# Second recurrence of a recurrent-memory attention and MLP gradient: rows loaded for two row groups at a time, one store of a block's gradient rows, and a new table of order

## The chip, the core and the metric

The kernel runs on one core of a Trainium2 chip. The metric is the time of one execution on the device in microseconds (us); the time before is 2793.9 us, the median of three runs (2793.06 to 2796.42). Below, PE is TensorE, ACT is ScalarE, DVE is VectorE, POOL is GpSimd, and SP is SyncE, whose queue issues nearly all of the transfers here. A trailing q (SPq) means the queue of that engine.

## The reference

The forward pass is a sum of a recurrent-memory attention and an MLP, both fed by the layer-normed input; the kernel returns the output and the gradients of ten inputs.

```
def _A_ref(x, mem0, Wq, Wk, Wv, Wo, seg_len):      # S 2048, Dm 512, H 32, Dh 128, M 8, seg 32
    mem = mem0
    for s in range(n_seg):                          # 64 segments, one after another
        h = jnp.concatenate([mem, x[:, s * seg_len:(s + 1) * seg_len, :]], axis=1)
        q, k, v = (jnp.einsum('btd,dhe->bhte', h, W) for W in (Wq, Wk, Wv))
        scores = jnp.where(mask, jnp.einsum('bhqe,bhke->bhqk', q, k) * scale, -1e9)
        o = jnp.einsum('bhqk,bhke->bhqe', _softmax(scores), v)
        o = jnp.einsum('bhte,hed->btd', o, Wo)
        mem = o[:, :M, :]
        outs.append(o[:, M:, :])
def _B_ref(x, w1, b1, w2, b2):                      # F 1792
    h = jnp.einsum('bsd,df->bsf', x, w1) + b1
    return jnp.einsum('bsf,fd->bsd', jnp.where(h > 0, h, 0) ** 2, w2) + b2
xn = _layernorm(x)
out = x + _A_ref(xn, ...) + _B_ref(xn, ...)
# returned: out and the vector-Jacobian product of out with grad_out, for all ten float inputs
```

The gradient runs through the 64 segments backwards, since the gradient of a segment's memory rows is a part of the gradient of the segment before.

## The kernel before

The program has four stages. The MLP with its gradients comes first; then the first recurrence (64 segments forwards); then the **second recurrence**, which walks the segments backwards and is the stage that the change touches; then the gradients of the attention weights (line 2159), a long run of matmuls over activations that the recurrences stored to DRAM.

In the second recurrence four segments make a block, and there are 16 blocks. For each segment there is a *step* (`chain`, called once for each segment) and `load`, which fetches the next segment's stored probabilities and activations. A step projects the incoming gradient rows (`proj`, line 864, weights `WB`, rows `PA`), forms three block-diagonal products (`bd_half`, line 974) whose results go through `XK`, multiplies them by the weights (`dh_part`, line 1774, weights `WA`) into the bank `R_A` (a slice of `XN`), and hands the memory rows to the next step by a small matmul, `gm` (line 1989), and a copy into `PA` (line 1992). So a step's last operations are: the last matmul of line 1774, the copy of the bank into `XN` on ACT (line 756), `gm`, the copy on DVE into `PA`, and the first `proj` of the next step. That loop through all 64 steps is the chain; all else in the stage is off it.

Each product of line 974 is evicted into `XK` by ACT or DVE (lines 756, 754), stored by SP as `S_GN<-XK`, turned on DVE (line 847) and read by line 1774. There are two buffers for three such products a step, so the third eviction of a step waits until the first one's store has landed.

Off the chain, once in a block, stand `l_pre` (lines 1809 and 930 are its matmuls, and line 864 with `PB`) and `l_post`. `l_post` goes over four row groups r, twice: it loads rows of `S_Q` (then of `S_GON`) and a padded table `S_DSL` (then `S_PL`) for each r (`load_x`), and multiplies two groups at a time (`mm`, line 1874). `blk_out` turns the block's gradient rows and stores them from `gNat` (a view of the tile `maskL`) to `S_GOA`.

Nothing is scheduled while the program runs. Every operation of the stage has a number in a table (`_BWD`, three tuples: the middle blocks, the first, the last), its due time in a block in nanoseconds times four, plus the engine that does it where there is a choice. `_Beat.run` sorts by these numbers, and each engine takes its instructions strictly in that order. SP too: a transfer that waits holds up every transfer behind it. A transfer takes one of eight semaphores in turn, so at most eight of SP's are under way.

Of the kernel before, what the change touches and what calls it, by code (L numbers as in the profile page):

```python
# [17 lines left out]
P = 128  # L18
# [179 lines left out]
        -546000, -2857200, -480000, -481200, 8879250, 1958400, 3563600, 3428400, 3358800, 10119849, 10143660,  # L198
        10143673, 10758308, 10758321, 6099600, 4994800, 2060400, 541200, 4580802, 7385202, 7385602, 8326802, 8824402,
        9103200, 9060400, 12611600, 12610400, 13626861, 13626873, -4334000, -3086798, -8438400, -12837600, -319597,  # L200
        -13471197, -16186000, 938000, 14389648, 14697884, 15015510, 15015520, 15015546, 15015568, 14915540, 14915552,
        14915565, 15155304, 15155317, 16495172, 12582691, 12582703, 14416771, 12582715, 12178775, 12178787, 12178799,
        13008887, 15015532, 15015557, 15015580, 15015593, 15246942, 16495186, 15246952, 15246964, 17158024, 17158036,
        15015664, 15015606, 16401514, 16401526, 16401538, 16401550, 16401562, 16401622, 16495198, 16495210, 17240374,
        17240386, 18255066, 17240398, 18255078, 15015619, 15015631, 15015643, 15015655, 16401575, 16401585, 16401597,
        16401611, 16944336, 16944349, 17240410, 17240423, 17240433, 17240446, 17240456, 17240517, 18235906, 18286922,
        18235916, 18235928, 18286932, 18286944, 23428480, 16401635, 16401645, 16401657, 16401671, 16401681, 16401693,
        16401707, 16401717, 17232288, 17783157, 17240469, 17240481, 17240493, 17240507, 18255090, 18255102, 18255114,
        18255127, 18255136, 18977533, 18569534, 18977546, 18569544, 18569556, 18977568, 18977580, 18977556, 19690537,
        19782597, 19690548, 19690562, 19782608, 19782622, 24547084, 17535616, 28380764, 13327536, 14420532, 24402643,  # L210
        24402655, 22194524, 19977928, -2821228, 7899676, 7373828, 3613352, -4696608, 8571312, 11740568, -69781,
        1558124, 4805860, 6352296, 7315404, 7733381, 10119800, 10119812, 10119824, 10119836, 2902029, 11447020,
        11447032, 11447044, 11447056, 11447070, 11447082, 12669054, 12669066, 13626802, 13626812, 13626824, 13626836,
        13626848, 13626884, 20930640, 20930652, 20930665, 23601096, 23601110, 24402664, 21843516, 21843528, 21843541,
        25147548, 25147561, 26802176, 18255151, 18255163, 23864939, 18255175, 20385003, 19204219, 17240531, 19148035,
        23864948, 23864961, 24748972, 24748985, 24715950, 26802190, 26947188, 27003728, 27104816, 27104828, 24749044,
        24402678, 25646686, 25646698, 25646710, 25646722, 25646734, 25646794, 26802202, 26802214, 26802226, 26802238,
        26802250, 26985338, 26802310, 24748999, 24749011, 24749023, 24749035, 25646747, 25646757, 25646769, 25646783,
        28361976, 28361989, 26802263, 26802275, 26802285, 26802297, 28614648, 28614661, 28362002, 28614710, 29609052,
        29609064, 29609076, 29609088, 30713416, 25646807, 25646817, 25646829, 25646843, 25646853, 25646865, 25646877,  # L220
        25646889, 27878264, 28843061, 27878278, 27878291, 27878301, 27878314, 26802321, 27541630, 26802335, 27083430,
        29000060, 29000073, 28843074, 29000146, 29609100, 29609112, 29609124, 29609136, 29000156, 29609149, 29609161,
        29609172, 29609210, 29609184, 29609222, 29609196, 25929872, 28805088, 21959012, 27793388, 30828719, 30828731,
        28733856, 29000084, 29609232, 29609244, 29609257, 31001308, 32005190, 32005200, 30458968, 31138912, 31138925,
        32272300, 32272313, 33163544, 29000099, 29000111, 29000123, 29000135, 28614675, 28614687, 28614699, 32237603,
        32237612, 32237637, 32237624, 32237649, 33139906, 33315202, 33982864, 33982876, 34779744, 34779756, 32237708,
        32281674, 32281686, 32281698, 32281710, 32281722, 32281734, 32281794, 33163558, 33163570, 33163582, 33163594,
        33810362, 33757294, 33810374, 32237663, 32237675, 32237687, 32237699, 32281747, 32281757, 32281769, 32281783,
        34296780, 34296793, 33163607, 33163619, 33163631, 33163641, 34923492, 34923505, 34296806, 34923566, 35592576,
        35621428, 35621440, 35621452, 35407824, 32281805, 32281817, 32281831, 32281843, 32359965, 32281853, 32281865,  # L230
        32281879, 34313164, 34989221, 34313177, 34313191, 34313201, 34313215, 33810386, 33810398, 33810410, 33810422,
# [1990 lines left out]
```

## Time and profile before

| What | Value |
|---|---|
| Median of three runs | 2793.9 us (2793.06 to 2796.42) |
| The profiled execution, its own time | 2801.72 us |
| Its span, first to last instruction | 2799.9 us |
| ACT busy in the whole span | 1288.3 us (46%) |
| DVE busy in the whole span | 1501.0 us (54%) |
| POOL busy in the whole span | 937.8 us (33%) |
| Bytes moved by transfers | 607.92 MB |
| Mean granted TensorE clock | 0.995 |

The times of the profile are from one execution, which took 7.8 us more than the median of the others. A busy share says how long an engine worked, not whether its waits matter: an idle engine costs something only where the engine that sets the end waits for it. In a row of waits the columns are the sum in us, how often, and the longest. In a row of a chain of waits they are the start in us, the length in us, and what held the chain there. In a row that groups instructions the columns behind the bar are busy us, mean ns of one, and the idle time before them with what ended it.

### The profile page before, as it was taken

How to read it: one execution, taken by the hardware profiler on the slowest of the kernel's cores; microseconds unless marked ns; L12 is line 12 of the kernel's file. 1: busy time of each engine (PE TensorE's matmuls, PEld its weight loads, DVE VectorE, ACT ScalarE, POOL GpSimd, SP SyncE). 2: the span in 40 equal slices, each digit the busy share in tenths (PEclk: the TensorE clock that was granted, in tenths of full speed). 3: DMA queues.
4: the chain of work that ended last, by engine and by line, in shares of the span. 5: the costliest groups of instructions: out<-in, count | busy, mean ns of one | idle time of the engine just before them, and what ended most of it. 6: DMA issues, size and time to landing. Idle time of an engine off the chain costs nothing.

```text
span 2799.9 us, 113515 instructions
## 1 busy us (share of the span) xinstructions
PE 2676.2 (96%) x47433; PEld 1560.2 (56%) x47617; DVE 1501.0 (54%) x4483; ACT 1288.3 (46%) x3070; POOL 937.8 (33%) x2624
## 2 busy tenths in 40 slices
PE   9999999999999998899999999999999899999999
PEld 7664566666666665655555555555555444444444
DVE  6555666666666666765555555555655402232322
ACT  4333555555555555556666666666666400000000
POOL 1103333233332333345444444454544301112211
PEclk9999999999999999999999999999999999999999
DMA  8748788788887764567989999989989898788861
GB/s 234 235 145 225 195 209 212 204 202 214 211 210 204 203 200 154 154 166 219 236 227 237 224 234 241 230 227 237 231 239 220 250 348 270 231 256 270 257 184 40
DMA packets 560278, 607.92 MB, mean 217 GB/s; under 512 B 231940, under 2 KB 361364, under 8 KB 557716
## 3 DMA queue, kind: packets, MB, share of 16 engines
q1 hardware_dynamic: 544580, 546.57, 73.0%
q0 software_dynamic: 15184, 54.08, 6.3%
q8 instruction: 373, 6.11, 1.0%
q14 instruction: 141, 1.16, 0.2%
HBM read 290.27 MB, written 272.12 MB: 201 GB/s over the span
## 4 chain that ended last, share of the span: by engine, by line
PE 43%; issue 7%; DMA 5%; DVE 2%; ACT 2%; POOL 1%; SPq 0%; POOLq 0%; ACTq 0%; DVEq 0%
PE ps L1774 13%; PE ps L2159 12%; PE ps L974 6%; PE ps L864 6%; PE ps L750 2%; DMA S_GN<-XK 2%; PE ps L1989 1%; DMA WA<-S_GN 1%; PE ps L1874 1%; PE ps L1934 1%; ACT XN L756 1%; PE ps L930 1%; DMA S_GNL<-dLN 0%; PE ps L1861 0%; POOL out_dram L2172 0%
## 5 line engine op out<-in xcount | busy, mean ns | idle before, releaser
L864 PE MATMUL ps<-WA,PA 128*32 128x512 bf16 x6144 | 367.9, 379 | 6.2 <-issue 2.9
L2159 PE MATMUL ps<-WA,WB 128*128 128x512 bf16 x1505 | 330.7, 379 | 2.2 <-DVE gwo L754 0.6
L1774 PE MATMUL ps<-WA,XK 128*32 128x512 bf16 x5120 | 307.1, 382 | 10.2 <-DVE XK L847 9.5
L864 PEld LDWEIGHTS <-PA 128*32 128x32 bf16 x8192 | 202.8, 96 | 196.1 <-DVE PA L1992 12.4
L2159 PEld LDWEIGHTS <-WB 128*128 128x128 bf16 x1896 | 185.5, 98 | 224.7 <-issue 0.9
L756 ACT CAST gwo<-ps 128x512 bf16<-128x512 f32 x64 | 33.2, 598 | 518.0 <-PE ps L2159 357.8
L990 POOL COPY BDA<-PB 32x128 bf16<-32x128 bf16 x538 | 155.9, 290 | 306.6 <-DVE PB L1563 253.1
L754 DVE CAST gwo<-ps 128x512 bf16<-128x512 f32 x64 | 40.0, 685 | 402.4 <-PE ps L2159 267.9
L756 ACT CAST XK<-ps 128x512 bf16<-128x512 f32 x379 | 211.0, 589 | 88.1 <-PE ps L974 65.8
L1774 PEld LDWEIGHTS <-XK 128*32 128x32 bf16 x5120 | 122.5, 97 | 146.2 <-DVE XK L847 31.1
L1774 PE MATMUL ps<-WA,XN 128*32 128x512 bf16 x2560 | 174.1, 381 | 2.4 <-DVE XN L847 2.1
L2170 POOL DMA_DIRECT2D out_dram<-gwo x96 | 71.4, 751 | 296.1 <-ACT gwo L756 264.3
L756 ACT CAST XA<-ps 128x512 bf16<-128x512 f32 x143 | 83.7, 590 | 151.3 <-PE ps L864 142.3
L756 ACT COPY XN<-ps 128x256 f32<-128x256 f32 (+2 forms) x215 | 93.6, 465 | 125.4 <-PE ps L1774 122.5
L864 PE MATMUL ps<-WB,PA 128*32 128x512 bf16 x2048 | 134.4, 385 | 10.0 <-issue 4.7
L847 DVE STREAM_TRANSPOSE XK<-XK 128x256 f32<-128x256 f32 x256 | 112.2, 442 | 44.6 <-ACT XK L756 38.6
L1432 PE MATMUL ps<-WB,OT 128*32 128x256 bf16 x4096 | 132.9, 275 | 3.2 <-DVE OT L847 1.6
L990 POOL COPY BDB<-PB 32x128 bf16<-32x128 bf16 x279 | 80.0, 287 | 163.5 <-DVE PB L1564 142.7
L990 ACT COPY BDA<-PB 32x128 bf16<-32x128 bf16 x430 | 127.1, 295 | 16.6 <-DVE PB L1563 7.6
L756 ACT CAST kN<-ps 128x512 bf16<-128x512 f32 x124 | 72.8, 587 | 128.5 <-PE ps L864 104.0
L996 POOL COPY BDA<-XA 32x256 bf16<-32x256 bf16 x256 | 104.5, 408 | 54.1 <-ACT BDA L990 17.1
L974 PEld LDWEIGHTS <-XK 128*128 128x128 bf16 x1536 | 94.5, 98 | 46.3 <-issue 15.9
(308 smaller groups left out, 5493.7 us busy)
## 6 DMA issues: line engine op xcount, KB each, us to landing
S_GN<-XK SPq DMA_DIRECT2D x192, 256.0 KB
WA<-S_GN SPq DMA_DIRECT2D x160, 256.0 KB
S_Q<-qN SPq DMA_DIRECT2D x64, 256.0 KB
S_K<-kN SPq DMA_DIRECT2D x64, 256.0 KB
S_V<-vN SPq DMA_DIRECT2D x64, 256.0 KB
S_ON<-oN SPq DMA_DIRECT2D x64, 256.0 KB
XA<-S_K SPq DMA_DIRECT2D x64, 256.0 KB
XA<-S_Q SPq DMA_DIRECT2D x64, 256.0 KB
```

Source lines behind the costliest of these rows:

```text
L750: nc.tensor.transpose(ps_ap, in_ap, ident[base:base + k, base:base + k])
L754: nc.vector.tensor_copy(out, in_)
L756: nc.scalar.copy(out, in_)
L847: self.plan.add({"DVE": 0.36}, lambda e, x=x: nc.vector.transpose(dst[:, x, :, :].rearrange("p i c r -> p (i c r)").bitcast(F32).rearrange ...
L864: nc.tensor.matmul(bk()[32 * j:32 * (j + 1), :], lhsT=win(dc), rhs=Wt(dc, c0), start=(dc == 0), stop=(dc == DC - 1), tile_position=(0, 32 ...
L974: nc.tensor.matmul(bv()[:, n * P:(n + 1) * P], lhsT=B_[:, i, :, :].rearrange("p j k -> p (j k)"), rhs=X[:, i, :], start=(y == 0 and n == 0 ...
L990: self.plan.add({"ACT": 0.31, "DVE": 0.2, "POOL": 0.31}, lambda e, j=j: {"ACT": nc.scalar.copy, "DVE": nc.vector.tensor_copy, "POOL": nc.g ...
L996: self.plan.add(cost or {"ACT": 0.4, "DVE": 0.27, "POOL": 0.42}, lambda e, j=j: {"ACT": nc.scalar.copy, "DVE": nc.vector.tensor_copy, "POO ...
L1432: nc.tensor.matmul(bk()[32 * t:32 * (t + 1), :], lhsT=tq(OTt, i, j), rhs=Wo[:, JQ * i + j, h * HB:(h + 1) * HB], start=(i == 0 and j < 2), ...
L1774: nc.tensor.matmul(bk()[32 * j:32 * (j + 1), :], lhsT=tq(XT, i, j), rhs=wtf(t, i, j), start=(first and i == 0), stop=(last and i == NI - 1 ...
L2159: nc.tensor.matmul(bks[n]()[:], lhsT=HNc[:, rc, dc * P:(dc + 1) * P], rhs=half_of(gns[y], hf), start=(y == 0), stop=(y == NRC - 1))
L2170: q.dma_start(outWs[t][dc * P:(dc + 1) * P, hf, :, j], wt[:].rearrange("p (i e) -> p i e", i=4))
```

## The change

Three edits in the second recurrence.

The eight tiles `XN` become slices of one tile `XNN`, in such an order that the row groups 0 and 1, and 2 and 3, lie side by side. `load_x` then issues one transfer for two row groups where it issued two, for the rows and for the padded table, in all blocks but one case (the last block's second pass, which has buffers elsewhere).

`blk_out` stores the four segments' rows with one transfer of the form 4x32x512 where it issued four of 32x512.

The table `_BWD` has new numbers throughout, for every operation of the stage: the order and, where there is a choice, the engine. The table of the first recurrence and the beat are as before.

```
@@ _BWD @@
-        -546000, -2857200, -480000, -481200, 8879250, 1958400, 3563600, 3428400, 3358800, 10119849, 10143660,
+        -546000, -2857200, -480000, -481200, 7206657, 1958400, 3563600, 3428400, 3358800, 11845705, 11733936,
...
@@
-    XN = [px.tile([P, HW], BF16, name="XN%d" % x) for x in range(8)]
+    XNN = px.tile([P, 8 * HW], BF16, name="XNN")
+    XN = [XNN[:, HW * x:HW * (x + 1)] for x in (0, 4, 1, 2, 6, 7, 3, 5)]
@@
-        xs = [XN[x] for x in (1, 4, 5, 7)]
+        xs = [XN[x] for x in (1, 7, 4, 5)]
@@ load_x @@
                 def load_x(r):
+                    if not (b == 0 and t == 2):
+                        if r % 2 == 0:
+                            two = lambda q, b=b, r=r: q[b, 32 * r:32 * (r + 2)].rearrange("(j r) v f -> (r v) j f", j=2)
+                            sg.dma(lambda: XNN[:, HW * (4 + r):HW * (6 + r)].rearrange("p (j f) -> p j f", j=2), lambda: two(big),
+                                   [(bn, s) for s in range(b * SPB, b * SPB + SPB)], xk[r] + xk[r + 1], lat=3.2)
+                            sg.dma(lambda: XN[6][:, r * NI * RL:(r + 2) * NI * RL].rearrange("p (j f) -> p j f", j=2), lambda: two(pad),
+                                   [(pn, s) for s in range(b * SPB, b * SPB + SPB)], yk[r] + yk[r + 1], lat=3.0)
+                        return
@@ blk_out @@
-            for v in range(SPB):
-                sg.dma(lambda v=v: S_GOA[b * P:(b + 1) * P, :].rearrange("(r v) d -> v r d", v=SPB)[v],
-                       lambda v=v: gNat[RA * v:RA * (v + 1)], ["gNat"], [])
+            sg.dma(lambda: S_GOA[b * P:(b + 1) * P, :].rearrange("(r v) d -> v r d", v=SPB), lambda: gNat, ["gNat"], [])
```

Since the line numbers move, the same places have other numbers in the program after the change: 864 becomes 861, 930 becomes 927, 1774 becomes 1772, 1989 becomes 1995, 810 becomes 807, 1781 becomes 1779.

On PE, at the end of the third step of a middle block, the program before has this order (`XK_2617` holds the turned products, `sel_97` and `XN_2621` are the operands of `gm`, `PA` the chain's rows and `WB` its weights):

```order
L1774 LDWEIGHTS XK_2617
L1774 MATMUL ps<-WA,XK_2617 32x512
L1989 MATMUL ps<-sel_97,XN_2621 32x8 x16
L864 LDWEIGHTS PA
L864 MATMUL ps<-WB,PA 32x512
```

And after the change, at the same place (`PB` holds the off-chain rows of `l_pre`):

```order
L861 LDWEIGHTS PB
L861 MATMUL ps<-WB,PB 32x512
L1995 MATMUL ps<-sel_97,XNN 32x8 x16
L861 LDWEIGHTS PA
L861 MATMUL ps<-WB,PA 32x512
```

Twelve off-chain projections, of which the first two rows are the last, have come between the step's last matmul of line 1774 and `gm`.

Also on PE, at the end of the fourth step of the block, the program before has the off-chain product of line 930 (which reads `dLN` and `XH`) ahead of `gm`:

```order
L930 LDWEIGHTS XH_2629
L930 MATMUL ps<-dLN,XH_2629 32x128
L1989 MATMUL ps<-sel_97,XN_2621 32x8 x16
L864 LDWEIGHTS PA
L864 MATMUL ps<-WB,PA 32x512
```

After the change it stands behind `gm`:

```order
L1772 LDWEIGHTS XK_2617
L1772 MATMUL ps<-WA,XK_2617 32x512
L1995 MATMUL ps<-sel_97,XNN 32x8 x16
L927 LDWEIGHTS XH_2622
L927 MATMUL ps<-XK_2616,XH_2622 32x128
```

So this `gm` has lost its filler, and the way from `gm` to the next projection has got one. Over steps 2 to 63, `gm` follows directly on line 1774 in 34 steps before and in 20 after; in 14 steps after, one for each middle block, line 927 stands between `gm` and the next projection.

On SP, at the end of a middle block, the program before issues these (the tiles `XN_2620` to `XN_2626` are row groups and the padded tables, `S_GOA<-maskL` is the store of gradient rows):

```order
L810 DMA S_R<-XN_2621 128x512
L1781 DMA_TRANSPOSE XA<-S_V 128x8x128
L810 DMA S_GN<-XK_2617 128x1024
L810 DMA dLN<-S_GNL 128x1024
L810 DMA XN_2620<-S_GON 128x1024
L810 DMA XN_2625<-S_PL 128x256
L810 DMA XN_2623<-S_GON 128x1024
```

Another padded table, the two other row groups with theirs, and the step's other two stores of `XK` follow. And after the change, at the same place:

```order
L807 DMA S_R<-XNN 128x512
L807 DMA S_GON<-XA 128x1024
L807 DMA S_GOA<-maskL 4x32x512
L807 DMA S_GN<-XK_2617 128x1024
L807 DMA XA<-S_P 128x320
L807 DMA XNN<-S_PL 128x2x256
L807 DMA dLN<-S_GNL 128x1024
L807 DMA XNN<-S_GON 128x2x1024 x2
L807 DMA XNN<-S_PL 128x2x256
L807 DMA S_GN<-XK_2617 128x1024 x2
```

The rows come in two transfers of 128x2x1024, back to back and ahead of the step's last two stores of `XK`, and the single store of 4x32x512 stands directly ahead of the step's first store of `XK`. Between two loads of `grad_out`, SP issues on average 72 transfers in a middle block before, and 61 after. In the whole program DVE evicts a product into `XK` 61 times after the change and 5 times before, ACT 323 and 379 times.

333 rows, old and new, of the table _BWD are left out of this document.

## The prediction

> **What bounds the kernel now.** I read the page first, then the busy times of the second recurrence, then what PE waits for in it, and last the chain of waits at the places that the new order touches. The page gives the span and the engines' shares:
>
> ```profile
> span 2799.9 us, 113515 instructions
> PE 2676.2 (96%) x47433; PEld 1560.2 (56%) x47617; DVE 1501.0 (54%) x4483; ACT 1288.3 (46%) x3070; POOL 937.8 (33%) x2624
> ```
>
> PE works 96% of the span, and the change takes no matmul away, so a gain has to come out of PE's remaining waits. The table of stretches (busy us of PE, PEld, DVE, ACT and POOL, then clock, DMA share and GB/s) shows how much there is. Its first row is the steady part of the second recurrence, its second the passage to the weight gradients.
>
> ```profile
> 1284.20:2176.30 892.10, 850.89 (x19364) 493.52 (x19362) 523.71 (x1655) 551.69 (x1345) 438.65 (x1365) 1.00 0.93 232
> 2230.00:2280.00 50.00, 42.98 (x270) 19.16 (x268) 3.38 (x6) 3.71 (x7) 4.03 (x6) 0.93 0.97 346
> ```
>
> In the steady part PE idles 892.1 - 850.9 = 41.2 us. DVE and ACT have over a third of the time free, while the transfers keep the DMA engines 93% busy. PE's order is the first limit, and transfers that come late are the second, with little room between. Whom PE waits for in that stretch:
>
> ```profile
> PE ps L1989 <- ACT XN L756: 13.8, 29, 0.5
> PE ps L1774 <- DVE XK L847: 5.5, 6, 2.0
> PE ps L864 <- DVE PA L1992: 4.1, 23, 0.2
> PE ps L1989 <- issue: 4.0, 3, 1.9
> PE ps L864 <- issue: 2.9, 3, 1.9
> PE ps L974 <- issue: 2.3, 2, 2.1
> PE ps L1861 <- issue: 1.0, 2, 0.8
> ```
>
> The first row is regular: 29 times `gm` waits 13.8/29 = 0.48 us for the copy of the bank on ACT. So is the third, 4.1/23 = 0.18 us each. The others are rare and long. The chain of waits shows one of the issues:
>
> ```profile
> 1457.58 1.89 issue
> ```
>
> The DMA view of the 1.7 us around its start (1456.5 to 1458.2) has this row among its queues:
>
> ```profile
> q8 instruction: 1, 0.02, 4.0%
> ```
>
> One 16 KB piece of the program came in on the instruction queue just ahead of the end of the wait. I read the issues as PE waiting for its program behind busy DMA engines; one case doesn't prove it. The waits on `XK` lead to transfers as well. The first row below is from ACT's waits in the steady part, the second from the list of its transfers:
>
> ```profile
> ACT XK L756 <- DMA S_GN<-XK: 13.9, 14, 2.8
> ```
>
> ```profile
> S_GN<-XK SPq DMA_DIRECT2D x168, 256.0 KB
> ```
>
> There are 168 stores, three a step, so this is 56 steps or 14 blocks. An eviction waited for 14 of them, one in twelve, 1.0 us each; 5.5 us of that reached PE.
>
> **The change, the order around gm.** The chain of waits shows a step's end without filler ahead of `gm`, and one with filler:
>
> ```profile
> 1372.42 3.60 PE ps L1774 x64
> 1376.04 0.38 ACT XN L756
> 1376.42 0.04 issue
> 1376.46 0.59 PE ps L1989 x32
> ...
> 1391.34 1.01 PE ps L930 x64
> 1392.36 0.29 PE ps L1989 x16
> 1392.67 0.18 DVE PA L1992
> 1392.85 0.04 issue
> 1392.90 1.25 PE ps L864 x17
> ```
>
> Where `gm` stands directly behind line 1774, PE has nothing to do while ACT copies (0.38 us and the hops). Where line 930 stands between, the copy is hidden, and what remains is the copy into `PA`, 0.18 us. The order gives 34 such bare ends before and 20 after, so 14 fewer: 14 x 0.48 = 6.7 us saved. That is what the new order plainly does in the third step of a block, and in the second it gains as much as it gives back in the fourth. The waits of 0.18 us come out even: a filled `gm` that the next projection follows directly is where they stand, 28 before; after, 42 are filled, and in some 14 of them the matmuls of `gm` are split by four other matmuls, which cover the hop. Both ends of this term: nothing, if the filler is missed elsewhere, and 13.8 us, if the whole row goes.
>
> **What the moved filler leaves bare.** In the fourth step, the first product for line 1774 that goes through `XK` now has less work behind it. Before, 16 matmuls of line 1774 and 64 of line 1809 came between its two halves; after, the second half follows at once, then eight more matmuls of line 974, then line 1774 asks for the first half. How long the way through `XK` takes, and what 16 matmuls of line 974 take, stand in the chain:
>
> ```profile
> 1351.41 6.72 DMA S_GN<-XK
> 1358.17 0.04 issue
> 1358.21 0.59 ACT XK L756
> 1358.83 0.46 DVE XK L847
> 1359.28 0.04 issue
> 1359.33 1.94 PE ps L1774 x32
> ...
> 1365.32 1.00 PE ps L974 x16
> ```
>
> From the eviction's release at 1358.17 to line 1774 at 1359.33 it is 1.16 us, against 1.00 us of cover: 0.16 us bare in each of 14 blocks, 2.2 us lost. The ends are 0 and 14 x 0.92 = 12.9 us, if each waits as long as the six waits on `XK` do now (5.5/6); I stay with 2.2, which the nearest rows give.
>
> **Fewer transfers.** A middle block issues 61 instead of 72, 15% fewer, with the same bytes. SP's time itself is worth nothing: no row has PE waiting for SP. What could shrink is the waits for late arrivals, 5.5 us on `XK` and 4.0 + 2.9 + 2.3 + 1.0 = 10.2 us of issues. The trace does not show how they depend on the number of transfers. One end is no gain, since the bytes stay and the engines are 93% busy with them; the other is all 15.7 us. They could grow by as much, since a pair is 512 KB in one piece ahead of the stores. I take 15% of them, 2.4 us saved, nearer to nothing because bytes fill the engines. No row has `mm` (line 1874) waiting for its loads, so that a pair has to wait for two free buffers is covered by the work ahead of `mm`, and I count it as nothing; without that cover it is a part of the same 15.7 us.
>
> **The single store.** The four stores of 32 KB become one of 128 KB, now directly ahead of the step's first store of `XK`. The trace has two stores of 128 KB that POOL issued within 10 us of each other, after the first recurrence. One has the new form, 4x32x512; the other goes out as 16x8x256. For each, the view by tile gives the issue and the landing:
>
> ```profile
> L810 POOL DMA_DIRECT2D S_HNA<-XH x1: 777/777/777, 1166.0 to 1166.0; - x1
> DMA to landing us min/median/max: 4.4/4.4/4.4
> ```
>
> ```profile
> L810 POOL DMA_DIRECT2D S_RO<-XH x1: 554/554/554, 1175.4 to 1175.4; - x1
> DMA to landing us min/median/max: 2.2/2.2/2.2
> ```
>
> The new form took 2.2 us longer. Nobody waits for this store itself. If all of it fell on the store behind, and that on PE, it would be 16 x 2.2 = 35 us; the other end is nothing. One store of `XK` in twelve is waited for now, and 5.5 of 13.9 us of such waits reach PE, so I take 16 x 2.2 x 1/12 x 0.4 = 1.2 us lost. The Trainium skill (DMA: Bandwidth & Descriptors, "Why a DMA increments its semaphore by 16 and not by 1") says that a transfer runs on the largest number of DMA engines up to 16 that divides the slowest dimension of both its sides: four engines for 4x32x512, sixteen for the stores that it replaces. The two landings agree with it; without it, as one transfer for four on the same engines, the store would cost nothing, and the sum would be 1.2 us less.
>
> **The engines' choices.** DVE takes 56 more evictions into `XK` from ACT. The page has the two engines' rows for a 128x512 eviction:
>
> ```profile
> L754 DVE CAST gwo<-ps 128x512 bf16<-128x512 f32 x64 | 40.0, 685 | 402.4 <-PE ps L2159 267.9
> L756 ACT CAST XK<-ps 128x512 bf16<-128x512 f32 x379 | 211.0, 589 | 88.1 <-PE ps L974 65.8
> ```
>
> Each is 96 ns longer on DVE, 5.4 us if all stood on the path; the handing over to DVE's turn falls away in return. I take nothing, with 5.4 as the other end.
>
> **The passage.** The last block's table is new too, but its bytes are the same, and the DMA share of 0.97 says that they set this stretch. I take nothing; the ends are 7.0 us (50.0 - 43.0) either way.
>
> **The sum** is -6.7 + 2.2 - 2.4 + 1.2 = -5.7 us, against an execution of 2801.7 us with its span of 2799.9. That execution was 7.8 us above the median, so I carry the difference, not the level: 2793.9 - 5.7 = **2788.2 us**.
>
> **The rivals.** *The gain is eaten.* The chain of a step has the same length, and filler that covers `gm` is missing ahead of line 1774; DVE's longer evictions of `XK` stand just there. For it: 1.16 us against 1.00 in the fourth step. Against it: DVE has 41% of the steady part free. With the 5.4 us on the path the sum is -0.3: 2793.6 us.
>
> *The single store delays the chain.* The store of `XK` behind it must land before the step's third eviction needs that buffer. From the point where it lands later than that, every block waits: 15 blocks with such a step x 1.0 us (13.9/14) = 15 us, all of it taken to reach PE, where 5.5 of 13.9 us do now. Without the gain from fewer transfers that is -6.7 + 2.2 + 15 = +10.5: 2804.4 us, slower. For it: the 6.72 us landing in the chain above, and the 4.4 us of the form. Against it: 11 of 12 stores land with time to spare.
>
> *The queue clears.* With 11 fewer transfers a block each store is issued earlier, the 5.5 us on `XK` go and half of the issues with them: -6.7 + 2.2 - 5.5 - 5.1 = -15.1: 2778.8 us. For it: the waits are rare, so a little room may end them; against it, the unchanged bytes. The Trainium skill (DMA: Bandwidth & Descriptors, "Rules for kernel authors") speaks for it, asking that transfers under 64 KB be joined since they are mostly overhead; no row here prices that overhead.
>
> **How the numbers follow.** What a measurement of this kernel can tell from no change is 0.2%, 5.6 us. My forecast stands at that edge, at -0.20%. I give it 0.44 (0.30 of it just beyond the edge, 0.14 short of it, between 2782 and 2792), the eaten gain 0.24 (0.04 faster, 0.17 the same, 0.03 slower), the delayed chain 0.20 (0.01 the same, 0.19 slower), the cleared queue 0.12, all faster. That is faster 0.46, the same 0.32, slower 0.22. The range goes from 2776, a little beyond the cleared queue, to 2804, the delayed chain: about a tenth is left out on each side, and the larger ends of the unknown terms lie there.
>
> **What would show it.** In the changed profile the row of `gm` (line 1995) waiting for ACT should have some 15 to 16 entries in the same steps for 29, and about 7 us for 13.8. A wait of line 1772 on line 844, the turn of `XK`, in each block's fourth step, 0.1 to 0.2 us long, would confirm what was laid bare; 0.5 us or more would be the eaten gain. Waits of ACT or DVE for `S_GN<-XK` should be 14 or fewer; some 15 or more, next to the single store, would be the delayed chain. The issues should stay between 8 and 13 us; under 6, the queue has cleared. The forecast is wrong if the stretch 2230 to 2280 changes by over 3 us, or if PE's busy time itself moves.

## The result and the profile after

The change makes the kernel slower. The median of four runs is 2824.8 us (2813.0 to 2826.4) against 2795.2 us (2793.1 to 2797.9) for four runs of the kernel before; the ratio is 1.0096, 95% interval 1.0067 to 1.0125, so some 27 us. That is outside the predicted range of 2776 to 2804. The profiled execution is a typical one this time (2824.7 us with a span of 2822.9). From the page of the changed kernel, its span and the engines' shares:

```profile
span 2822.9 us, 113454 instructions
PE 2675.3 (95%) x47433; PEld 1573.8 (56%) x47617; DVE 1529.0 (54%) x4546; ACT 1250.4 (44%) x2962; POOL 955.5 (34%) x2669
```

PE's busy time is the same as before to a microsecond, 2675.3 for 2676.2 us, so the loss stands in PE's waits; that the busy time did not move is itself two effects that cancel, as the clock below shows. The table of stretches of the changed kernel shows where (busy us of PE, PEld, DVE, ACT, POOL, then clock, DMA share, GB/s). The first row is the same 14 blocks of the second recurrence, the second the passage to the weight gradients:

```profile
1289.40:2202.70 913.30, 850.45 (x19362) 506.13 (x19360) 550.43 (x1718) 513.87 (x1232) 456.46 (x1412) 0.99 0.96 226
2256.00:2306.00 50.00, 44.47 (x273) 19.96 (x275) 3.38 (x6) 3.71 (x7) 6.54 (x9) 0.93 1.04 376
```

The 14 blocks take 913.3 us for 892.1, and PE idles 62.9 us in them for 41.2: the 21 us are there. In the passage PE is busy 1.5 us more of the 50 us. The blocks begin 5.2 us later; that much is scatter, since in the traces of kernels with the old order they begin anywhere from 1283.2 to 1291.6 us. The waits of PE of the changed kernel in the 14 blocks (us in all, how many, the longest):

```profile
PE ps L1772 <- DVE XK L844: 9.8, 16, 2.8
PE ps L1995 <- ACT XNN L753: 7.2, 15, 0.5
PE ps L1995 <- issue: 4.8, 4, 1.7
PE ps L1772 <- issue: 4.7, 3, 1.9
PE ps L971 <- issue: 4.2, 4, 1.9
PE ps L1880 <- issue: 3.9, 3, 2.1
PE ps L1940 <- issue: 3.9, 3, 1.8
PE ps L861 <- issue: 3.6, 5, 1.0
PE ps L971 <- POOL XK L987: 3.3, 10, 1.3
PE ps L747 <- ACT XA L753: 3.1, 12, 0.3
PE ps L1867 <- issue: 3.1, 2, 1.9
PE ps L861 <- DVE PA L1998: 2.0, 10, 0.2
```

Three things stand here. The bare ends at `gm` (line 1995) are halved, 7.2 us for 13.8, as the order promised. The issues add up to 28.7 us (with a row of 0.5 that is left out), where they were 12.5 before (10.2 in the rows of the prediction and 2.3 in smaller ones). And line 1772 waits longer for the turn of `XK`, 9.8 us for 5.5.

**What an issue is.** The chain of waits of the changed kernel has this one (start, length, what held the chain):

```profile
1747.51 0.55 PE ps L1880 x16
1748.06 1.67 issue
1749.73 0.35 PE ps L1995 x14
```

The DMA view of 1746.3 to 1748.9 us has among its queues:

```profile
q8 instruction: 1, 0.02, 2.6%
```

So far this is one case more, like the one of the prediction. The places settle it. I numbered PE's records (matmuls and weight loads) from the start of the program and took every wait of the kind issue over 0.3 us in the 14 blocks. Four of the 24:

```
PE starts  waited  line   number   modulo 256   last 16 KB packet   granted clock
again at   us                                   on q8 ended         0.50 from
1537.39    1.86   L971    59710       62          1536.02           1538.41
1552.07    1.93   L1867   60222       62          1550.68           1552.06
1606.28    1.81   L1940   62525       61          1605.06           1606.67
1749.73    1.67   L1995   68669       61          1748.21           1750.03
```

All 24 lie on the same number modulo 256 (61 or 62, since a record is missing here and there), and so do all 11 of the kernel before: every 256th instruction of PE, 1.1 to 1.7 us behind the end of a 16 KB packet on the instruction queue. PE's program comes in blocks of 256 instructions, of which PE works off one in some 5.9 us. From the time when PE enters a block to the end of the packet that brings the next one it took 2.95 us before and 3.61 us after on average (152 blocks each), though a packet itself takes 1.1 us in both (the median). I read this as a packet that waits its turn on busy DMA engines; where that takes longer than PE works at its block, PE stands. In the changed kernel 11 of the 152 landed more than 6 us after, in the kernel before one. The Trainium skill (Runtime: NRT & Kernel Launch, "Instruction fetch mechanics") gives the same 16 KiB blocks of 256 instructions, fetched one ahead on a DMA queue, and calls the cost of crossing a boundary mostly hidden; here it is 28.7 us in 913, so under this DMA load the measurement differs.

**What follows a long wait.** The last column above is the clock. In the 14 blocks of the changed kernel the granted clock drops to 0.50 for 3.41 us five times, in those of the kernel before twice. All 18 traces of this case have 48 such drops in these blocks (four of them last 6.83 us), and each begins either during a wait of PE or at most 2.3 us behind its end; none of these waits is shorter than 0.98 us. Not each long wait brings a drop: of the changed kernel's ten waits over 1.5 us, five have one. So the lower clock of the changed kernel comes with its long waits. A drop of 3.41 us costs half of that, 1.7 us of work, and this stands in PE's busy time. With it taken off, PE is busy 847.3 to 848.0 us in the 14 blocks of the five traces with the old order in the table below, and 840.6 to 842.4 in the six with the new one. The new order took some 5.6 us off PE's own work (why stays open), and three more drops gave 5.1 us back. Together with 21.7 us more of idle time this is the 21 us.

**What the wait on XK is.** The chain of the changed kernel at the longest of them:

```profile
1375.84 8.45 DMA S_GN<-XK
1384.29 0.03 issue
...
1384.41 0.70 DVE XK L751
...
1385.14 0.46 DVE XK L844
1385.59 0.04 issue
1385.64 1.47 PE ps L1772 x21
```

The eviction may overwrite the buffer only when the store of `S_GN` has read it, and this store took 8.45 us. The 16 waits of the row are of two kinds. Five are long, 0.44 to 2.78 us and 7.3 us in all; four of them hang on a store of `S_GN` like this one, and one is put down to the load `XA<-S_P`. The other eleven are 0.19 to 0.26 us long, 2.4 us in all, each in a block's fourth step behind an eviction on ACT and a turn on DVE.

**What SP waits for.** SP never has more than eight transfers under way at once, in any trace of this case (a transfer counted from its issue to the last update of its semaphore before the semaphore's next use). Before it issues a ninth it waits for an earlier one. The largest such rows of the kernel before, among SP's waits in the 14 blocks:

```profile
SPq L810 <- DMA S_GN<-XK: 8.8, 17, 1.8
SPq L810 <- DMA XN<-S_GON: 5.3, 9, 1.6
SPq L810 <- DMA XN<-S_Q: 3.6, 8, 0.8
```

and of the changed kernel:

```profile
SPq L807 <- DMA S_GON<-XA: 2.6, 1, 2.6
SPq L807 <- DMA S_GOA<-maskL: 0.9, 1, 0.9
SPq L807 <- DMA S_GN<-XK: 0.8, 2, 0.4
```

All rows of the kind add up to 28.2 us before (21.3 in a second trace of it, before_again) and 6.4 after. That looks like a gain, and the experiments show that it is not one.

### The profile page after: what moved, and what is told of

Its sections match the earlier page's. It is cut to its first block, busy times and chain, and to the rows that moved or that the text cites. A ratio compares the mean times of both kernels' runs of the same rounds, so it can differ in the third digit from the quotient of the medians.

```text
span 2822.9 us, 113454 instructions
## 1 busy us (share of the span) xinstructions
PE 2675.3 (95%) x47433; PEld 1573.8 (56%) x47617; DVE 1529.0 (54%) x4546; ACT 1250.4 (44%) x2962; POOL 955.5 (34%) x2669
## 4 chain that ended last, share of the span: by engine, by line
PE 37%; issue 7%; DMA 5%; DVE 2%; ACT 2%; POOL 1%; SPq 0%; POOLq 0%; DVEq 0%; ACTq 0%
PE ps L1772 12%; PE ps L2163 11%; PE ps L861 5%; PE ps L971 4%; PE ps L747 2%; DMA S_GN<-XK 1%; DMA WA<-S_GN 1%; PE ps L1880 1%; PE ps L1995 1%; PE ps L1940 1%; PE ps L1867 1%; PE ps L927 1%; ACT XK L753 0%; POOL out_dram L2176 0%; DVE XNN L751 0%
## 5 line engine op out<-in xcount | busy, mean ns | idle before, releaser
L1772 PE MATMUL ps<-WA,XK 128*32 128x512 bf16 x5120 | 323.8, 382 | 16.0 <-DVE XK L844 11.1
L753 ACT CAST XK<-ps 128x512 bf16<-128x512 f32 x323 | 185.0, 587 | 121.2 <-PE ps L971 69.7
L1772 PE MATMUL ps<-WA,XNN 128*32 128x512 bf16 x2560 | 163.5, 382 | 2.6 <-issue 1.8
L753 ACT CAST XA<-ps 128x512 bf16<-128x512 f32 x156 | 90.3, 589 | 132.6 <-PE ps L861 129.9
L753 ACT COPY XNN<-ps 128x256 f32<-128x256 f32 (+1 forms) x204 | 86.7, 458 | 130.6 <-PE ps L1772 116.1
L751 DVE COPY XNN<-ps 128x512 bf16<-128x512 bf16 (+1 forms) x100 | 45.3, 453 | 150.5 <-PE ps L747 150.5
L844 DVE STREAM_TRANSPOSE XK<-XK 128x256 f32<-128x256 f32 x256 | 110.8, 442 | 20.8 <-ACT XK L753 14.9
L971 PEld LDWEIGHTS <-XK 128*128 128x128 bf16 x1536 | 95.9, 98 | 46.4 <-issue 21.3
L1430 PEld LDWEIGHTS <-OT 128*32 128x32 bf16 x4096 | 101.0, 97 | 33.2 <-DVE OT L844 17.4
```

The lines of the kernel that those rows point to most:

```text
L751: nc.vector.tensor_copy(out, in_)
L753: nc.scalar.copy(out, in_)
L844: self.plan.add({"DVE": 0.36}, lambda e, x=x: nc.vector.transpose(dst[:, x, :, :].rearrange("p i c r -> p (i c r)").bitcast(F32).rearrange ...
L971: nc.tensor.matmul(bv()[:, n * P:(n + 1) * P], lhsT=B_[:, i, :, :].rearrange("p j k -> p (j k)"), rhs=X[:, i, :], start=(y == 0 and n == 0 ...
L1430: nc.tensor.matmul(bk()[32 * t:32 * (t + 1), :], lhsT=tq(OTt, i, j), rhs=Wo[:, JQ * i + j, h * HB:(h + 1) * HB], start=(i == 0 and j < 2), ...
L1772: nc.tensor.matmul(bk()[32 * j:32 * (j + 1), :], lhsT=tq(XT, i, j), rhs=wtf(t, i, j), start=(first and i == 0), stop=(last and i == NI - 1 ...
```

## The experiments

The change has three parts: the order, the pair loads and the single store. Each experiment takes one apart, from the changed kernel (a_) or from the kernel before (b_); except in a_evact, PE, ACT, DVE and POOL keep their order row for row, and only what SP issues differs. The table gathers most of them. Ratios are to the kernel before on the same chip. The last three columns are of the one profiled execution, over its 14 blocks: PE's issue waits, the mean time from PE's entering a block to the landing of the next one, and the share of the time with more than 1,600 KB of SP's transfers under way (from issue to landing; transposing transfers, whose size the trace does not give, count as nothing). The edits below are shortened.

```
kernel       order rows    pads    stores  median   ratio [95%]              issue  fetch  >1600 KB
before       old   single  single  4       2795.2   1                         12.5   2.95   0.4%
before_again old   single  single  4       2789.9   (one run)                  9.3   2.86   0.9%
b_store1     old   single  single  1       2801.9   1.0006 [0.9994, 1.0019]   11.8   2.85   0.9%
b_pairs      old   pairs   pairs   4       2809.5   1.0042 [1.0025, 1.0060]   13.5   3.00   5.0%
b_both       old   pairs   pairs   1       2807.1   1.0046 [1.0031, 1.0061]   17.9   3.06   6.8%
a_table      new   single  single  4       2824.3   1.0108 [1.0087, 1.0128]   12.0   3.39   5.1%
a_singles    new   single  single  1       2809.3   1.0053 [1.0033, 1.0073]   12.4   3.39   5.0%
a_padpair    new   single  pairs   1       2816.5   1.0066 [1.0044, 1.0089]   24.9   3.50   6.4%
after        new   pairs   pairs   1       2824.8   1.0096 [1.0067, 1.0125]   28.7   3.61   7.6%
a_store4     new   pairs   pairs   4       2841.5   1.0159 [1.0135, 1.0182]   32.3   3.71  10.8%
a_slot2      new   pairs+  pairs+  1       2810.2   1.0038 [1.0024, 1.0052]   19.4   3.55   6.2%
```

**a_table, both merges undone under the new order.** Where one pair stood, SP issues two single loads back to back; where the store stood, four:

```diff
-    sg.dma(lambda: XNN[...], lambda: two(big), ...)
+    A({"SP": T_DMA}, lambda e: [nc.sync.dma_start(xx[x], quad_rows(big, b, x)) for x in (r, r + 1)], ...)
...
-    sg.dma(lambda: S_GOA[...].rearrange("(r v) d -> v r d", v=SPB), lambda: gNat, ...)
+    A({"SP": T_DMA}, lambda e: [nc.sync.dma_start(S_GOA[...][v], gNat[RA * v:RA * (v + 1)]) for v in range(SPB)], ...)
```

> The changed kernel with both merges undone and the new order of slots kept: at each slot of a pair SP issues the two single transfers back to back, at the slot of the one store the four stores; the order on PE, ACT, DVE and POOL is that of the changed kernel row for row. Theory T (the new order itself costs the 27 to 29 us): 2820 to 2827 us, PE's waits of the kind issue at 24 us or more from 1410 to 2145. Theories S (the store on four engines) and P (the pairs in pieces of 512 KB) both: 2785 to 2797 us, issue waits back at about 12 us as before the change.

Measured: 2824.3 us, which is what theory T expected, but with issue waits of 12.0 us, which is what the others expected. The time is right for another reason. Two rows of PE's waits of a_table, and one of DVE's:

```profile
PE ps L1867 <- DVE dLN L751: 16.2, 12, 2.4
PE ps L1772 <- DVE XK L844: 8.7, 16, 3.1
```

```profile
DVE XK L844 <- DMA dLN<-S_GNL: 18.4, 12, 2.5
```

The new order puts the store directly ahead of the loads with which the next step begins. Four issues there make the load of `dLN` late, and 16.2 us of that reach PE. So this kernel alone does not tell how dear the order is; the next two do.

**a_singles and a_store4, one merge undone at a time.** Each has one half of the edit above.

> The changed kernel with the pair loads alone undone (two single transfers back to back at the pair's slot); one store and new order kept. Theory P: 2790 to 2800 us. Theory S or T: 2818 to 2827 us. If the cause is shared, the time lies between.

> The changed kernel with the one store alone undone (four stores of 32x512 back to back at its slot); pair loads and new order kept. Theory S: 2790 to 2800 us. Theory P or T: 2818 to 2827 us.

Measured: 2809.3 us, between the ranges, as for a shared cause, and 2841.5 us, above both. Three rows of PE's waits of a_singles:

```profile
PE ps L1772 <- DVE XK L844: 10.6, 21, 3.0
PE ps L1867 <- DVE dLN L751: 5.7, 7, 1.4
PE ps L1772 <- ACT dLN L753: 3.3, 7, 1.6
```

With one store the wait of line 1867 falls from 16.2 to 5.7 us. The pairs cost from 1.0053 to 1.0096 with one store and from 1.0108 to 1.0159 with four: 0.43% (these two intervals just overlap) and 0.51%, 12 to 14 us. The single store, at this place, saves 0.55 to 0.63%, 15 to 18 us. The order with one store and single loads costs 0.53%, 15 us. Theory S falls: the store gains, it doesn't cost. No theory alone holds; order and pairs share the loss.

The 14 blocks of a_singles show what the pairs do in the new order:

```profile
1285.10:2183.50 898.40, 842.05 (x19358) 502.22 (x19356) 552.61 (x1718) 513.23 (x1232) 458.48 (x1413) 1.00 0.97 230
```

From here to the changed kernel it is 14.9 us. PE's issue waits rise by 16.3 us, but its idle time only by 6.5 (62.9 for 56.4), since the other waits shrink by 9, most of all those for a late `dLN`. The other 8.4 us stand in PE's busy time and fit the clock: a_singles has no drop in these blocks, and five drops are 8.5 us.

**b_both, b_store1 and b_pairs, the merges under the old order.** The kernel before with the single store at the place of the first of the four (others issue nothing), with the pairs at the place of the even row group, and with both.

> The kernel before with its own order of slots and both merges: the pair stands at the slot of its first row group, the store at the first slot of the four, the other slots issue nothing; PE, ACT, DVE and POOL keep the order of before. Theory T: 2790 to 2798 us, no change. Theories S and P together: 2812 to 2825 us, with PE's issue waits from 1410 to 2145 at 24 us or more instead of 12.

> The kernel before with the one store alone, at the first of its four slots; loads and order of before. If one store is worth its 15 to 17 us under any order (as between a_table and a_singles): 2778 to 2786 us. If it was worth that only because the new order puts all four at one place ahead of the load of dLN: 2792 to 2800 us. If four DMA engines with 32 KB each hold up what is behind (theory S): 2803 us or more.

> The kernel before with the pair loads alone, at the slot of the first row group; four stores and order of before. If pairs delay PE's instruction fetch under any order: 2803 to 2813 us, as b_both, with PE's issue waits over the 14 middle blocks at 17 us or more, and the fetches asked for near a pair landing 0.4 us or more later than those near a single load in the kernel before. If they do so only in the new order: 2792 to 2800 us.

Measured: 2807.1, 2801.9 and 2809.5 us; b_both lies between the two ranges, b_store1 2 us above the middle one, b_pairs within its first. The pairs cost 0.42% here too, 12 us, so they do so under either order. The expectation on their issue waits came out half: 13.5 us instead of 17 or more with the pairs alone, 17.9 with both. That on the landing held. Where PE enters a block within 4 us behind the issue of a load of rows, the next block lands after 3.87 us in b_pairs and 3.98 in b_both, for 3.20 and 3.00 in the two traces of the kernel before; in all other places it is 2.8 us in each of the four.

The trace of b_pairs does not show the 12 us themselves:

```profile
1291.60:2177.20 885.60, 849.70 (x19360) 493.94 (x19356) 523.80 (x1655) 550.93 (x1345) 440.90 (x1364) 1.00 0.94 234
```

PE idles 35.9 us here, as it does in the blocks of b_store1 (36.0) and before_again (35.6). But this execution was the fastest of twelve, 2801.3 us for a median of 2809.5. In b_both, a typical one, PE idles 43.1 us. So how the delay of the packets comes to 12 us under the old order is shown in part only.

The store alone changes nothing (0.9994 to 1.0019): its gain under the new order is that of four issues crowded at one place, which the old order, with the four apart, never had.

**before_again, a second profile of the kernel before.**

> The kernel before once more, for a second profile to set the others beside: 2790 to 2800 us. If its waits of the kind issue on PE over the 14 middle blocks are again 10 to 15 us and those of line 1774 on the turn of XK 4 to 7 us, the comparison with the first profile stands; if they are above 20 us, the growth of the issue waits with the change is only scatter between executions.

Measured: 2789.9 us, with issue waits of 9.3 us and 2.6 us on the turn of `XK`, all three a little under the expected ranges and far from the 20 us of mere scatter. The execution of the first profile lay 7.8 us above the median; beside this one, with 883.1 us for the 14 blocks, the changed kernel loses 30 us there instead of 21.

```profile
1283.20:2166.30 883.10, 847.54 (x19363) 491.81 (x19359) 523.07 (x1655) 551.39 (x1345) 437.81 (x1363) 1.00 0.95 234
```

**a_slot and b_slot, then a_slot2 and b_slot2: why a pair is dear.** A pair has the bytes of two loads at the place of two loads. What it does away with is one of eight places. These kernels put a transfer that nobody needs behind each pair (or, in the kernel before, behind each single load of rows), so that the places are as scarce as with single loads:

```diff
+    TNN = px.tile([8, 32], BF16, name="TNN")
+    TN = [TNN[:, 2 * x:2 * x + 2] for x in range(16)]
...
-    sg.dma(lambda: XNN[...], lambda: two(big), ...)
+    A({"SP": T_DMA}, lambda e: [nc.sync.dma_start(XNN[...], two(big)), nc.sync.dma_start(TN[n % 16], mem0flat[0:8, 0:2])], ...)
```

> The changed kernel, its pair loads kept as they are, and behind each of them one transfer of 8x32 (512 bytes) into a tile that nobody reads, so that a pair takes two of SP's transfers again, as the two single loads did. Theory F (what a pair does away with is the limit on transfers under way: in the kernel before SP waited for its own earlier transfers 27 us in 14 blocks, in the changed one 6): SP's waits for DMA rise to 12 us or more, PE's issue waits over the 14 blocks fall from 28 to 18 us or less, and the time to 2806 to 2816 us. Theory G (a load of 512 KB in one piece itself delays the fetch): issue waits at 25 us or more, 2818 to 2832 us.

> The kernel before, unchanged in order and transfers, with one transfer of 512 bytes behind each single load of rows in the middle blocks, which tightens the limit on transfers under way. Theory F: PE's issue waits over the 14 blocks fall from 9 to 13 us to 8 us or less; the time is 2790 to 2800 us, since what SP then waits itself is given back. Theory G: issue waits unchanged, and the time 2797 to 2803 us for 8 more issues in a block.

These two used one tile of 512 bytes where the lines above, which are of a_slot2, have 16 places, and each small transfer waited for the one before. Of SP's waits in a_slot:

```profile
SPq L1850 <- DMA TN<-in_A_mem_dram: 110.1, 67, 4.6
```

Issue waits fell to 7.1 and 8.4 us, but the times were 2876.4 and 2849.8 us, since SP itself had become late. They lie outside all ranges and say only that a slower SP gives fewer issues. The next two write to 16 places in turn:

> a_slot mended: the small transfer behind each pair (32 bytes now) goes to one of 16 places in turn, so that SP no longer waits for the small transfer before it, which cost a_slot 102 us of SP's time; it only takes one of the eight transfers that may be under way. Theory F (the pairs loosen that limit): the mean under way in bytes falls from 979 KB to 960 KB or less, issue waits over the 14 blocks from 28 to 18 us or less, the time to 2806 to 2818 us. Theory G (one piece of 512 KB): issue waits at 25 us or more, 2820 to 2832 us.

> b_slot mended in the same way, on the kernel before. Theory F: 870 KB or less under way, issue waits of 8 us or less, 2788 to 2798 us. Theory G: issue waits of 9 to 13 us, 2796 to 2804 us for the added issues.

Measured for a_slot2: 2810.2 us, 1.0038 where the changed kernel has 1.0096, with the same pairs and useless transfers on top. Its 14 blocks, and the first of SP's waits for transfers (32.3 us in all, where the changed kernel has 6.4):

```profile
1290.00:2189.00 899.00, 843.36 (x19359) 502.94 (x19357) 552.38 (x1718) 513.34 (x1232) 456.10 (x1412) 1.00 0.98 230
```

```profile
SPq L807 <- DMA XNN<-S_GON: 9.4, 10, 1.6
SPq L807 <- DMA dLN<-S_GNL: 7.2, 8, 1.6
SPq L1332 <- DMA S_GON<-XA: 5.6, 5, 2.3
```

The time is where theory F expected it, and a load in one piece of 512 KB (theory G) can't explain it alone, since the pairs are as they were. Issue waits fell from 28.7 to 19.4, a little short of the expected 18. The delay near a load of rows is gone: where PE enters a block within 4 us behind its issue, the next block lands after 3.96 us, as in a_singles (3.96), where the changed kernel has 4.54; of blocks that land after more than 6 us there is one instead of 11. The clock drops once instead of five times. One expectation missed: the mean under way did not fall (995 KB for 979). What fell is the peak, from 2,176 KB at most to 1,872. The share of time above 1,600 KB fell little, and with the transposing transfers counted at 256 KB each (the size of `XA<-S_V`) hardly at all, from 11.9% to 11.3. Nor do the issue waits follow that share throughout the table: they are 12 us at 0.4% (before) as at 5% (a_table, a_singles), and higher only above 5%. So the limit on transfers under way is shown to be what the pairs loosen; that it acts through this share is not.

b_slot2 marks the other side: on the kernel before, issue waits came to 8.5 us (12.5 and 9.3 in its two traces) and the mean under way to 857 KB (886 before), about as theory F expected, but the time rose to 2815.1 us (1.0063, 1.0045 to 1.0082), neither theory's range. There SP's added waits made other transfers late, among them rows of PE waiting 9.8 us for `XA` and 9.2 for `XK`. Scarcer places pay where bursts are the trouble, not everywhere.

**a_padpair, pairs of pads alone.** Rows single, pads (64 KB each) in pairs.

> The changed kernel with the loads of rows (256 KB each) single again, back to back, and the loads of pads (64 KB each) in pairs. If the cost of pairs lies in the large ones: as a_singles, 2806 to 2814 us, with issue waits of 10 to 16 us. If it goes with the number of transfers saved, half of which are pads: between a_singles and the changed kernel, 2815 to 2820 us.

Measured: 2816.5 us, between a_singles and the changed kernel, with issue waits of 24.9 us: the small pairs loosen the limit too. It speaks for theory F, though its interval (1.0044 to 1.0089) overlaps those of both.

**a_evact, the evictions back on ACT.** In the eviction of `dN`:

```diff
-    lambda: bv()[:], [(dst[0], g)], prio, EV_F)
+    lambda: bv()[:], [(dst[0], g)], prio, {"ACT": 0.49} if 0 < self.plan.at[0] < TC - 1 and dst[0][0:2] == "dN" else EV_F)
```

> The changed kernel with the four evictions of dN2 and dN1 of a block that the new order gives to DVE put back on ACT, at the same slots; nothing else moves. If it is DVE's place that makes line 1772 wait 9.8 us on the turn of XK: that wait falls to 5 us or less and the time by 4 to 8 us, to 2816 to 2821 us. If it is the store of S_GN, which must have read the buffer before either engine may write it: the wait stays between 8 and 12 us, now behind ACT's eviction, and the time within 2821 to 2828 us.

Measured: 2832.1 us (1.0122, 1.0102 to 1.0143), outside both. Of its PE waits:

```profile
PE ps L1773 <- DVE XK L844: 30.6, 24, 3.8
```

The wait on the turn tripled, while the issue waits fell from 28.7 to 18.6 us. As far as this trace and a median 7 us higher go, DVE's taking these evictions is a gain of the new table; the intervals overlap, so the gain in time is not shown. I had the sign wrong in one theory and no effect in the other.

**a_sing_dln, a_late and a_sing_late: what is left of the order.** One transfer is moved on SP, by a shift of its number: the load of `dLN` 2.1 us up, or the store 51 us back. Divided by four, the numbers of the table are hundredths of a nanosecond, not nanoseconds (the beat is 6498399 for a block of some 65 us), so the shifts are 210000 and 5100000.

```diff
-    heapq.heappush(heap, (self.beat * o.blk + x // 4, o.idx, e))
+    heapq.heappush(heap, (self.beat * o.blk + x // 4 + shift, o.idx, e))
```

> a_singles (new order, one store, single loads) with the load of dLN from S_GNL moved up on SP past the load of XA and the two loads of pads; nothing else moves. If what is left of the new order's cost is that this load is late (line 1867 waits 5.7 us on DVE's dLN and line 1772 3.3 us on ACT's): those two waits fall under 2 us and the time to 2798 to 2803 us. If the cost is elsewhere: 2806 to 2813 us.

> The changed kernel with its one store moved back by 51 us in the order, to the place (in the next block) where the kernel before had the first of its four; on SP alone, nothing else moves. If the store's place among the loads at a block's end is part of what makes that step slow: 2810 to 2819 us, with the issue waits or the waits on the turn of XK lower by 5 us or more. If it is not: 2821 to 2829 us.

> a_singles (new order, single loads) with the one store moved back by 51 us as in a_late. If the place of the store is what is left of the new order's cost: 2797 to 2805 us. If it is not: 2807 to 2814 us.

Measured: 2808.8 us (1.0035, 1.0023 to 1.0048), 2819.2 us (1.0077, 1.0062 to 1.0091) and 2811.1 us (1.0042, 1.0025 to 1.0058). With the load of `dLN` moved up, line 1867 no longer waits for it, but another row grew, and the time stayed. PE's waits of a_sing_dln:

```profile
PE ps L1773 <- ACT dLN L754: 7.9, 9, 1.8
PE ps L1773 <- DVE XK L845: 6.5, 16, 1.1
```

So its cost is elsewhere, as the second range said. With the store out of the way (a_late) the wait on `XK` of the changed kernel fell from 9.8 to 3.1 us, and issue waits rose from 28.7 to 32.4; the time is at the upper end of the range for a part of the cost. a_sing_late lies in the range for no effect. All three intervals overlap those of the kernels they were made from. No single transfer that I moved carries the order's 15 us.

## Why the prediction was wrong

**Fewer transfers (-2.4 us) is the step that failed first.** It took the issues for a matter of how many transfers there are, and expected 15% less of them. The reading of an issue was right, a late piece of the program; the sign was wrong. Issue waits became 28.7 us for 12.5. Fewer transfers let SP run further ahead, and the pairs cost 12 to 14 us instead of the 2.4 saved, as b_pairs, a_singles against the changed kernel, and a_table against a_store4 show. The step's own far end, 15.7 us lost, was close, but it was given too little weight: nothing in the chances stood for it, and the only rival about the queues was that they clear.

**The order was priced on PE alone.** The term around `gm` is right: 15 entries and 7.2 us were measured for a forecast of 15 to 16 and about 7. But the same table also moved SP's transfers, and the prediction followed of these only the store. With single loads and one store the order costs 15 us net of that gain (a_singles). It is seen in PE's rows of waits, which add up to 51.4 us there for 37.4 before: late `dLN` (5.7 and 3.3 us, for 0.3), a longer wait on the turn of `XK` (10.6 us, for 5.5 and 2.6 in the two traces before), line 747 on `XA` (3.6 for 1.2) and line 971 on ACT, DVE and POOL (4.2, for no row before), against 9 us less at `gm` and `PA`; the issues are the same (12.4 for 12.5). PE's next block of program lands after 3.39 us under the new order even with single loads, for 2.9 under the old, and the time above 1,600 KB is 5% for less than 1%: the order crowds the transfers of a block's end. That this crowding is the cause was not tried by itself, and moving one transfer at a time did not undo it.

**What the moved filler leaves bare (+2.2 us)** came as it was forecast: eleven waits of some 0.2 us in the blocks' fourth steps, 2.4 us in all, for 14 of 0.16. What the sum did not have is the other five waits of that row, 7.3 us, four of them on a store of `S_GN` that has not landed. The waits of ACT and DVE for that store are 14 in all, for 15 before, but 1.5 us long instead of 1.0.

**PE's busy time and the clock** have no term in the sum. The new order's 5.6 us less of work and the 5.1 us of three more drops of the clock cancel in the total, so the prediction's sign of being wrong, a busy time that moves, did not show: luck.

**The single store (+1.2 us)** is not contradicted: under the old order it is worth 0.06%, within a measurement's scatter. The rival that it delays the chain did not happen; four stores at its new place cost 15 to 18 us, in a_table by a late `dLN`. The rule of four engines, which gave it its price, is not refuted by this, since nobody waits for the store.

**The engines' choices (0)** were, if anything, a gain: a_evact without four of them a block is 0.26% slower, but the intervals overlap. **The passage (0)** moved by 1.5 us, within the 3 us of its sign.

Of the four cases none came true. The eaten gain and the cleared queue had the wrong mechanism; the delayed chain had the right sign with the wrong carrier.

## What to carry to other kernels

Joining transfers takes away a brake: if the issuing queue stops at a fixed number under way, fewer and larger ones can put more bytes ahead of everything else, here the program's own code among it. A wait that this makes long can cost twice, in itself and in the slower clock that may follow it. Before merging loads that nobody waits for, look whether the queue's waits for its own transfers are what keeps the DMA engines free. And when a table moves a whole order, price the transfers it moves as well as the matmuls.

## What the runs showed of the hardware

- PE's unexplained waits fall on every 256th of its instructions, 24 of 24 in the changed kernel and 11 of 11 before, 1.1 to 1.7 us behind the end of a 16 KB packet of the instruction queue.
- Each of 48 drops of the granted clock to 0.50 began during a wait of PE of 0.98 us or more, or at most 2.3 us behind its end; 44 lasted 3.41 us, four 6.83. Of the changed kernel's ten waits over 1.5 us, five had one.
- SP had at most eight transfers under way in every trace, with 852 issues in 14 blocks as with 1,114.
- A transfer of 32 bytes that nobody needs, behind each pair, made the changed kernel some 16 us faster, measured by the ratios to the kernel before (1.0038 for 1.0096).
- Executions of one kernel scatter with the granted clock: b_pairs took 2801.3 us at 0.996 and 2821.4 at 0.992. Over the runs of all these kernels 0.001 of clock goes with 2.4 us. The changed kernel ran at 0.9935 on average, 71 runs of the kernel before at 0.9950, so some 3.5 us of the loss go with a lower clock. In the 14 blocks it is lower for the drops behind its long waits, five for two.
